# Placing VectorE's sum for the last down product behind the block's last output sum

## The chip, the cores and the metric

The kernel runs on one core of a Trainium2 chip. The metric is the device time of one execution in microseconds (us). One execution was also taken by the hardware profiler; its page and its trace are what this document reads. Engines are named as there: PE is TensorE's matmuls, PEld its weight loads, DVE is VectorE, ACT ScalarE, POOL GpSimd, SP SyncE. L12 is line 12 of the kernel.

## What is computed

Two stages follow each other: a filter in the frequency domain along the sequence of each of 8 batches, and a two-layer network with a hardswish between its layers on every one of the 8 x 3008 = 24064 tokens.

```python
X = np.fft.rfft(x, axis=1)                    # x: (8, 3008, 256)
Y = X * (filt_r + 1j * filt_i)[None]
x = np.fft.irfft(Y, n=3008, axis=1).reshape(24064, 256)
h = x @ w_in                                  # (256, 2048)
g = h * np.clip(h + 3.0, 0.0, 6.0) / 6.0
out = g @ w_out                               # (2048, 256)
```

All data is float32.

## The kernel before, in words

The network runs in 47 blocks of 512 tokens (`NBLK`, k = 0 to 46). A block runs through its 2048 hidden columns in 8 parts (`NP`, p = 0 to 7) of 256. One step of the main loop is one (k, p): it does the up products of (k, p) and the down products of the part before it, (kd, pd). The filter of the next batches is cut into units (`b_unit`, `f_unit`, `y_unit`, `bi3_unit`, `n_unit` and others), and a plan made ahead of the loop sets which unit runs in which step, at one of three places in it, `do(0)`, `do(1)` and `do(2)`. The order of instructions on every engine is the order in which the program issues them; nothing is reordered by a scheduler.

Each 2 x 2 block product is done with seven products in place of eight (in Strassen's manner), so sums are needed in front and behind.

- Up, products by their weights: A11, S1 and A12 (`up_1`), S2 and S4 (`up_2`), S3 (`up_3`), A22 (`up_5`). They accumulate in two PSUM tiles, `al` and `be`. VectorE makes h0 from them in `up_2b` (L790) and the upper half of h1 in `up_3` (L795); ScalarE copies the lower half of h1 (L804) and makes the two relus (L809). A22 writes into `al`, so its weight load waits until h1's addition has read it.
- Hardswish: `hswish(k, p, 0)` and `hswish(k, p, 1)` (L814) write G11 with G3's first content, and G12 with G22. The second is issued in the next step, at the head of `g_sums`.
- VectorE's sums for the down products: `g_sums` makes G1 (L821), then G3 and G2 (L822); `g_last` makes G4 = G12 - G2 (L827). G4 is read by down product 3 alone.
- Down: seven products numbered 1 to 7, each of two matmuls of 128 columns, each of these done as two loads and two matmuls in the trace (L843). In one step they come as 1; 2 and 4; 5 and 6; 7 and 3. They accumulate over the 8 parts of a block in four PSUM banks, `po0` to `po3`: products 1 and 4 in bank 0, 2 and 6 in bank 1, 5 in bank 2, 7 and 3 in bank 3. Products 1, 2, 5 and 7 open their banks in the first part of a block.
- The block's sums: when a block's last part is through, ScalarE and VectorE take the four banks apart into the output tile `o`. `out_1` (ScalarE, L900), `out_2` and `out_3` (VectorE, L909 and L914) run in the step with pd = 7; `out_4` (two VectorE sums, L918 and L919, and a GpSimd sum, L920) and `out_5` (one VectorE sum, L923, that reads the second half of bank 3) run in the step after it, whose pd is 0. `out_5` ends with `store(kd - 1)`, which issues the DMAs of that block's output from SP. There are 45 such steps with kd > 1; they have p = 1.

`g_last` has two places. In a step that is `late(i)` it comes directly behind h1's addition, in others in front of product 1. `late` holds for every step with p = 1 or 2, and for steps behind one with a heavy unit:

```python
        def late(i):
            return i % NP in (1, 2) or any(fn in HEAVY for place in range(3) for fn, a in plan.get((i - 1, place), ()))
```

So in the 45 steps VectorE's order is: hswish 1 of the part before, G1, G3 and G2, the two sums of `out_4`, h0, h1, G4 (`g_last`), `out_5`, hswish 0. TensorE's order is: `up_1`, units of `do(0)`, product 1, `up_2`, products 2 and 4, `up_3`, products 5 and 6, units of `do(1)`, `up_5` (A22), products 7 and 3.

GpSimd makes the seven sums of the next block's inputs in `t_sums` (L760), whenever ScalarE has copied them (`ready`), and the one sum of `out_4`.

The main loop (in the function that the diff touches) and what calls it:

Of the kernel before, what the change touches and what calls it, by code (L numbers as in the profile page):

```python
# [182 lines left out]
def kernel(  # L183
# [582 lines left out]
    def up_1(k, p):  # L766
        t = st["xt", k]
        al = psU.tile([P, 512], FP32, name="al")[:, 0:256]
        be = psU.tile([P, 512], FP32, name="be").rearrange("p (a n) -> p a n", a=2)
        s = hp.tile([P, 2, 256], FP32, name="s")  # L770
        s5 = hp.tile([P, 256], FP32, name="s5")
        product(al, p, A11, t[:, F1, :], start=True)
        product(be[:, 1, :], p, S1, xb(k, 0, 1), start=True)
        product(be[:, 0, :], p, A12, t[:, F4, :])
        nc.scalar.activation(out=s[:, 0, :], in_=al, func=AXT.Copy)  # L775
        nc.scalar.activation(out=s5, in_=be[:, 1, :], func=AXT.Copy)  # L776
        st["up"] = al, be, s, s5
# [10 lines left out]
    def up_2b(k, p):  # L788
        al, be, s, s5 = st["up"]
        nc.vector.tensor_tensor(out=st["h"][0].rearrange("p (a n) -> p a n", a=2), in0=be, in1=s, op=ALU.add)  # L790
# [26 lines left out]
    def g_sums(k, p):  # L817
        hswish(k, p, 1)
        g = st["g", k, p]
        v = nc.vector  # L820
        v.tensor_tensor(out=g[:, G1, :], in0=g[:, G3, :], in1=g[:, G22, :], op=ALU.add)  # L821
        v.tensor_tensor(out=g[:, G3:G2 + 1:2, :], in0=g[:, G3:G1 + 1, :],  # L822
                        in1=g[:, G11:G11 + 1, :].broadcast_to([P, 2, 256]), op=ALU.subtract)

    def g_last(k, p):
        g = st["g", k, p]
        nc.vector.tensor_tensor(out=g[:, G4, :], in0=g[:, G12, :], in1=g[:, G2, :], op=ALU.subtract)  # L827
# [7 lines left out]
    def down(k, p, *prods):  # L835
        g = st["g", k, p]
        if p == 0 and 1 in prods:
            st["po", k] = [psO.tile([P, 2, 2, P], FP32, name="po%d" % i) for i in range(4)]
        for n in prods:
            bank, part = BANK[n]  # L840
            a, w = DOWN[n]
            for u in range(2):
                nc.tensor.matmul(st["po", k][bank][:, part, u, :], g[:, a, ts(u, P)], w_out[p][:, w, :],  # L843
                                 start=(p == 0 and n in OPENS and u == 0), stop=(p == NP - 1 - (k == LAST)),
                                 skip_group_check=True)

    def last_down():
        p, v, add = NP - 1, nc.vector.tensor_tensor, ALU.add
        g, o = st["g", LAST, p], st["o", LAST][0]
        hswish(LAST, p, 1)  # L850
        ps = [psF.tile([P, 512], FP32, name="psf", tag="f") for t in range(2)]
        for i, a in ((0, G11), (1, G12)):
            for t in range(2):
                for u in range(2):
                    nc.tensor.matmul(ps[t][:, ts(u, D)], g[:, a + t, ts(u, P)],
                                     w_out[p][:, 2 * i:2 * i + 2, :].rearrange("p j m -> p (j m)"),
                                     start=i == 0 and u == 0, stop=i == 1, skip_group_check=True)
        out_4(LAST)
        v(out=o_at(LAST, 0, 1), in0=st["po", LAST][3][:, 1, :, :], in1=o_at(LAST, 0, 1), op=add)
        for t, qs in ((0, (nc.sync, nc.gpsimd, nc.scalar)), (1, (nc.sync, nc.scalar))):  # L860
            both = o[:, t, :, :].rearrange("p u d -> p (u d)")
            v(out=both, in0=ps[t], in1=both, op=add)
            store_last(t, qs)
# [6 lines left out]
    def plain_up(p):  # L870
        st["g", 0, p] = gp.tile([P, 7, 256], FP32, name="g")
        st["h"] = [psU.tile([P, 512], FP32, name=n) for n in ("al", "be")]
        for i in range(2):
            for d in range(2):
                nc.tensor.matmul(st["h"][i], w_in[p][:, 2 * d + i, :], xn[:, d, :, 0:PAIRS], start=d == 0, stop=d == 1)  # L875
            relu(i)
            hswish(0, p, i)

    def plain_down(p, tokens=(0, 1)):
        g = st["g", 0, p]  # L880
        if p == 0:
            st["po", 0] = [psO.tile([P, 2, 2, P], FP32, name="po%d" % i) for i in range(2)]
        for t in tokens:
            for u in range(2):
                for i, a in ((0, G11), (1, G12)):
                    nc.tensor.matmul(st["po", 0][t][:, u, :, :].rearrange("p a m -> p (a m)"), g[:, a + t, ts(u, P)],  # L886
                                     w_out[p][:, 2 * i:2 * i + 2, :].rearrange("p j m -> p (j m)"),
                                     start=p == 0 and u == 0 and i == 0, stop=p == NP - 1, skip_group_check=True)
# [14 lines left out]
    def o_at(k, t, d):  # L903
        return st["o", k][0][:, t, :, ts(d, P)]
# [17 lines left out]
    def out_5(k):  # L922
        nc.vector.tensor_tensor(out=o_at(k, 0, 1), in0=st.pop(("po", k))[3][:, 1, :, :], in1=o_at(k, 0, 1), op=ALU.add)  # L923
        store(k)
# [20 lines left out]
    def store(k):  # L945
        o = st["o", k][0]
        nc.sync.dma_start(o_d[ds(k * PAIRS, PAIRS)].rearrange("(u p) d -> p u d", p=P), o[:, 1, :, :])
        for u, p, m, b_, j, a in runs(k):
            for h in range(1 if j else 2):
                nc.sync.dma_start(raw(out, b_ * N + row(j, h, a), [[NC * D, m], [1, D]]), o[p:p + m, h, u, :])  # L950
        for b_, r, j, m, na in BACK.get(k, ()):
            to, half = out.offset + (b_ * N + N - j) * D, D // 2
            a0, a1 = ([[D, m], [-NC * D, na], [1, D]], [[NA * D, m], [D, na], [1, D]]) if m > 1 else (
                [[half, 2], [-NC * D, na], [1, half]], [[half, 2], [D, na], [1, half]])
            nc.sync.dma_start(bass.AP(tensor=out.tensor, offset=to, ap=a0),
                              bass.AP(tensor=o_d.tensor, offset=o_d.offset + r * D, ap=a1))
# [21 lines left out]
    with tc.manual_schedule():  # L978
# [207 lines left out]
        def late(i):  # L1186
            return i % NP in (1, 2) or any(fn in HEAVY for place in range(3) for fn, a in plan.get((i - 1, place), ()))

        items = [(k, p) for k in range(NBLK) for p in range(NP)]
        for i in range(len(items) + 1):  # L1190
            up = i < len(items)
            k, p = items[min(i, len(items) - 1)]
            dn = i > 0
            kd, pd = items[i - 1]
            def do(place):
                for fn, a in plan.get((i, place), ()):
                    fn(*a)

            if k == 0:
                plain_up(p)  # L1200
                do(0)
                if dn:
                    plain_down(pd)
                do(1)
                do(2)
                continue
            if not up:
                last_down()
                break
            up_1(k, p)  # L1210
            ends = k == LAST and p == NP - 1
            do(0)
            last_plain = dn and kd == 0
            dn = dn and kd > 0
            if dn:
                g_sums(kd, pd)
                if not late(i):
                    g_last(kd, pd)
                down(kd, pd, 1)
            if up:  # L1220
                up_2(k, p)
            if dn and pd == 0 and kd > 1:
                out_4(kd - 1)
            if up:
                up_2b(k, p)
            if dn:
                down(kd, pd, 2, 4)
                if pd == NP - 1:
                    out_1(kd)
            if up:  # L1230
                up_3(k, p)
                if dn and late(i):
                    g_last(kd, pd)
            if dn:
                down(kd, pd, 5, 6)
            if up:
                up_4(k, p)
            if ends:
                out_1(k)
            if last_plain:  # L1240
                plain_down(pd, (0,))
            if dn and pd == 0 and kd > 1:
                out_5(kd - 1)
            if up:
                hswish(k, p, 0)
                do(1)
            if up:
                up_5(k, p)
            bi3_copies()
            if last_plain:  # L1250
                plain_down(pd, (1,))
                plain_out()
            if dn:
                if pd == NP - 1 or ends:
                    out_2(kd)
                down(kd, pd, 7, 3)
                if pd == NP - 1 or ends:
                    out_3(kd)
            do(2)
# [30 lines left out]
```

## Time and profile before

| what | value |
|---|---|
| median of 3 runs | 2656.8 us (2656.7 to 2656.96) |
| the profiled execution's own time | 2656.55 us |
| its span in the profile | 2654.7 us |
| mean granted TensorE clock | 0.999 |
| DVE L827 (`g_last`), 367 times | 414 / 415 / 943 ns (least, median, most) |
| DVE L923 (`out_5`), 45 times | 411 / 419 / 424 ns |
| DVE L795 (h1), 368 times | 425 ns mean |
| POOL L760, sums of `xn` / of `xt` | 757 / 932 ns mean |

The page gives busy times and shares of the span by engine, the chain of work that ended last, and groups of instructions by line with their mean length and the idle time ahead of them. Two more views are used. The waits list who waited for whom, in total, how often, and the longest. The timeline lists instructions in order of time: start from the span's beginning, length, engine, line, operation, output and inputs, how many instructions are merged in the row, and in brackets the idle time in front of it with what ended it. Lengths of neighbours can overlap by some hundredths of a microsecond, since an engine starts an instruction while the one before is finishing. The ends of matmuls are modelled, so TensorE's pace is better read from the starts of its weight loads.

### The profile page before, as it was taken

To read this page: it belongs to the slowest core of one execution; us is meant where nothing else is said; L and a number is where in the kernel's file an instruction comes from. 1 tells how busy PE (TensorE), PEld (TensorE's weight loads), DVE (VectorE), ACT (ScalarE), POOL (GpSimd) and SP (SyncE) were. 2 spreads that over 40 slices of the span, in tenths; PEclk is the share of its full clock that TensorE was granted. 3 is DMA by queue.
4 is the path that set the end of the run, shared out by engine and by line. 5 is a ranking of instruction groups with operands and counts; after the bars stand their busy time and mean duration, and the time that the engine had idled before them with its cause. 6 is when DMAs were issued, how large, how long until landed. Compare 5 with 4: busy or idle time off the path is not lost.

```text
span 2654.7 us, 54856 instructions
## 1 busy us (share of the span) xinstructions
PE 2638.6 (99%) x21872; PEld 2334.1 (88%) x21872; DVE 2038.2 (77%) x3602; ACT 1298.6 (49%) x2682; POOL 484.3 (18%) x707
## 2 busy tenths in 40 slices
PE   8999999999999999999999999999999999999999
PEld 6688888889889898898988988889888888999998
DVE  7878767887678876788767887688877878766666
ACT  4554454444544444444444544545445444454554
POOL 2242021120211102121021210211112120111110
PEclk9999999999999999999999999999999999999999
DMA  9732234112241133411333112331223321110000
GB/s 248 219 92 71 72 84 115 52 32 82 79 116 52 32 85 81 111 52 36 80 88 104 52 37 80 89 103 52 56 61 88 103 56 48 48 43 22 19 20 25
DMA packets 130646, 198.29 MB, mean 75 GB/s; under 512 B 21538, under 2 KB 97408, under 8 KB 130198
## 3 DMA queue, kind: packets, MB, share of 16 engines
q1 hardware_dynamic: 115165, 150.12, 20.7%
q0 software_dynamic: 14656, 44.16, 6.0%
q8 instruction: 173, 2.83, 0.5%
q14 instruction: 83, 0.68, 0.1%
q10 hardware_dynamic: 569, 0.50, 0.1%
HBM read 122.43 MB, written 83.98 MB: 78 GB/s over the span
## 4 chain that ended last, share of the span: by engine, by line
PE 97%; DVE 2%; DMA 1%; issue 0%; ACT 0%; SPq 0%; POOL 0%; POOLq 0%; DVEq 0%
PE po L843 43%; PE al L764 24%; PE be L764 18%; PE psn L704 2%; PE psf L539 1%; PE psf L480 1%; PE po L886 1%; PE be L599 1%; PE psf L599 1%; PE be L480 1%; PE psf L583 0%; DMA w_all<-in_x_dram 0%; PE al L875 0%; PE be L875 0%; DVE g L814 0%; PE po L548 0%
## 5 line engine op out<-in xcount | busy, mean ns | idle before, releaser
L843 PEld LDWEIGHTS po<-w_all,g 128*128 128x128 f32 x10276 | 1366.4, 191 | 121.1 <-issue 20.3
L843 PE MATMUL po<-w_all,g 128*128 128x128 f32 x10276 | 1396.7, 276 | 1.2 <-DVE g L814 0.6
L809 ACT ACTIVATE r<-h,half_c 128x512 f32<-128x512 f32 x736 | 531.0, 721 | 334.1 <-DVE h L790 322.0
L764 PE MATMUL al<-xt,w_all 128*128 128x256 f32 x2208 | 659.7, 381 | 0.1
L814 DVE SCALAR_TENSOR_TENSOR g<-r,h 128x512 f32<-128x512 f32 x736 | 530.1, 720 | 159.8 <-ACT r L809 144.7
L764 PE MATMUL be<-xt,w_all 128*128 128x256 f32 x1472 | 437.8, 379 | 0.0
L790 DVE TENSOR_TENSOR h<-be,s 128x512 f32<-128x512 f32 x368 | 253.8, 690 | 157.3 <-PE be L764 148.6
L764 PEld LDWEIGHTS al<-xt,w_all 128*128 128x128 f32 x2208 | 335.5, 192 | 1.0 <-issue 0.5
L764 PEld LDWEIGHTS be<-xt,w_all 128*128 128x128 f32 x1472 | 279.8, 190 | 37.8
L760 POOL TENSOR_TENSOR xt<-xn 128x256 f32<-128x256 f32 x184 | 135.9, 757 | 876.7 <-ACT xn L686 842.6
L804 ACT ACTIVATE h<-al 128x256 f32<-128x256 f32 x368 | 141.0, 383 | 299.8 <-PE al L764 299.8
L795 DVE TENSOR_TENSOR h<-al,s 128x256 f32<-128x256 f32 x368 | 156.3, 425 | 157.4 <-PE al L764 154.1
L822 DVE TENSOR_TENSOR g<-g 128x512 f32<-128x512 f32 x367 | 261.3, 712 | 12.6
L785 ACT ACTIVATE s<-al 128x256 f32<-128x256 f32 x368 | 141.1, 383 | 211.9 <-PE al L764 210.4
L764 PE MATMUL al<-xn,w_all 128*128 128x256 f32 x736 | 226.1, 389 | 0.0
L776 ACT ACTIVATE s<-be 128x256 f32<-128x256 f32 x368 | 141.1, 383 | 172.2 <-PE be L764 172.2
L764 PE MATMUL be<-xn,w_all 128*128 128x256 f32 x736 | 218.9, 379 | 0.0
L821 DVE TENSOR_TENSOR g<-g 128x256 f32<-128x256 f32 x367 | 167.5, 456 | 12.6
L775 ACT ACTIVATE s<-al 128x256 f32<-128x256 f32 x368 | 140.8, 383 | 71.7 <-PE al L764 71.7
L764 PEld LDWEIGHTS be<-xn,w_all 128*128 128x128 f32 x736 | 139.9, 190 | 18.9
L827 DVE TENSOR_TENSOR g<-g 128x256 f32<-128x256 f32 x367 | 154.6, 421 | 2.5
L920 POOL TENSOR_TENSOR o<-p,o 128x256 f32<-128x256 f32 x46 | 36.8, 799 | 602.8 <-DVE o L918 557.4
(171 smaller groups left out, 1933.5 us busy)
## 6 DMA issues: line engine op xcount, KB each, us to landing
t<-g_tmp SPq DMA_DIRECT2D x184, 120.0 KB
t<-z_tmp SPq DMA_DIRECT2D x42, 512.0 KB
g_tmp<-t POOLq DMA_DIRECT2D x72, 256.0 KB, 5.5
z_tmp<-t POOLq DMA_DIRECT2D x120, 144.0 KB, 3.4
o_tmp<-o SPq DMA_DIRECT2D x46, 256.0 KB
xs<-in_x_dram SPq DMA_DIRECT2D x60, 192.0 KB
ft<-in_filt_r_dram SPq DMA_DIRECT2D x168, 64.0 KB
ft<-in_filt_i_dram SPq DMA_DIRECT2D x168, 64.0 KB
```

What stands on the lines that cost most here:

```text
L764: nc.tensor.matmul(ps, w_in[p][:, w, :], x, start=start, stop=stop, skip_group_check=True)
L776: nc.scalar.activation(out=s5, in_=be[:, 1, :], func=AXT.Copy)
L785: nc.scalar.activation(out=s[:, 1, :], in_=al, func=AXT.Copy)
L790: nc.vector.tensor_tensor(out=st["h"][0].rearrange("p (a n) -> p a n", a=2), in0=be, in1=s, op=ALU.add)
L795: nc.vector.tensor_tensor(out=st["h"][1][:, 256:512], in0=al, in1=s5, op=ALU.add)
L804: nc.scalar.activation(out=st["h"][1][:, 0:256], in_=al, func=AXT.Copy)
L809: nc.scalar.activation(out=r, in_=st["h"][i], func=AXT.Relu, bias=half_c, scale=1.0 / 6.0)
L814: nc.vector.scalar_tensor_tensor(out=st["g", k, p][:, o:o + 2, :].rearrange("p a n -> p (a n)"), in0=st["r", i], scalar=1.0, in1=st["h"][i ...
L821: v.tensor_tensor(out=g[:, G1, :], in0=g[:, G3, :], in1=g[:, G22, :], op=ALU.add)
L822: v.tensor_tensor(out=g[:, G3:G2 + 1:2, :], in0=g[:, G3:G1 + 1, :], in1=g[:, G11:G11 + 1, :].broadcast_to([P, 2, 256]), op=ALU.subtract)
L827: nc.vector.tensor_tensor(out=g[:, G4, :], in0=g[:, G12, :], in1=g[:, G2, :], op=ALU.subtract)
L843: nc.tensor.matmul(st["po", k][bank][:, part, u, :], g[:, a, ts(u, P)], w_out[p][:, w, :], start=(p == 0 and n in OPENS and u == 0), stop= ...
```

## The change

In the 45 steps that have `out_5` in them, `g_last` is issued behind `out_5` (and behind the store that `out_5` ends with) in place of directly behind h1's addition. Every other step keeps its order. On VectorE the order h1, G4, `out_5`, hswish 0 becomes h1, `out_5`, G4, hswish 0. No instruction is added or left out.

```diff
@@ -1229,7 +1229,7 @@
                     out_1(kd)
             if up:
                 up_3(k, p)
-                if dn and late(i):
+                if dn and late(i) and not (pd == 0 and kd > 1):
                     g_last(kd, pd)
             if dn:
                 down(kd, pd, 5, 6)
@@ -1241,6 +1241,7 @@
                 plain_down(pd, (0,))
             if dn and pd == 0 and kd > 1:
                 out_5(kd - 1)
+                g_last(kd, pd)
             if up:
                 hswish(k, p, 0)
                 do(1)
```

## Prediction

> **What bounds the kernel now.** First the page: busy shares, then the chain that ended last.
>
> ```profile
> PE 2638.6 (99%) x21872; PEld 2334.1 (88%) x21872; DVE 2038.2 (77%) x3602; ACT 1298.6 (49%) x2682; POOL 484.3 (18%) x707
> PE 97%; DVE 2%; DMA 1%; issue 0%; ACT 0%; SPq 0%; POOL 0%; POOLq 0%; DVEq 0%
> ```
>
> TensorE is the bound, so only its waits matter. Busy time hides short ones; the waits of the weight loads (PEld) show them:
>
> ```profile
> PEld po L843 <- PE po L843: 10.3, 32, 0.3
> ```
>
> 32 times a load of a down product stood 0.32 us. The timeline of the weight loads in block 9 (start, length, engine, line) says where:
>
> ```profile
> 593.98 0.30 PEld L764 LDWEIGHTS al<-xn,w_all 128*128 128x128 f32 x2
> 594.60 0.97 PEld L843 LDWEIGHTS po<-w_all,g 128*128 128x128 f32 x8 [0.32 <-PE po L843]
> 595.49 0.30 PEld L764 LDWEIGHTS al<-xt,w_all 128*128 128x128 f32 x2
> ...
> 600.32 0.30 PEld L764 LDWEIGHTS al<-xn,w_all 128*128 128x128 f32 x2
> 600.64 1.08 PEld L843 LDWEIGHTS po<-w_all,g 128*128 128x128 f32 x8
> 601.64 0.30 PEld L764 LDWEIGHTS al<-xt,w_all 128*128 128x128 f32 x2
> ```
>
> al<-xn is product A22 (up_5), the eight loads are down products 7 and 3, the next al<-xt opens the next step. In the step after (p=2) it goes 600.32, 600.64, 601.64: 1.32 us. In step p=1, where the change is, it goes 593.98, 594.60, 595.49: 1.51 us. Product 7's load comes 0.30 late, and 0.19 of it stays, since a load otherwise starts 0.11 before its matmul can. VectorE at that place:
>
> ```profile
> 593.40 0.42 DVE L795 TENSOR_TENSOR h<-al,s 128x256 f32<-128x256 f32 x1 [0.56 <-PE al L764]
> 593.74 0.41 DVE L827 TENSOR_TENSOR g<-g 128x256 f32<-128x256 f32 x1
> 594.07 0.42 DVE L923 TENSOR_TENSOR o<-po,o 128x256 f32<-128x256 f32 x1
> 594.40 0.88 DVE L814 SCALAR_TENSOR_TENSOR g<-r,h 128x512 f32<-128x512 f32 x1
> 595.89 1.22 DVE L814 SCALAR_TENSOR_TENSOR g<-r,h 128x512 f32<-128x512 f32 x1 [0.61 <-ACT r L809]
> ...
> 599.04 0.68 DVE L790 TENSOR_TENSOR h<-be,s 128x512 f32<-128x512 f32 x1
> 599.73 0.42 DVE L795 TENSOR_TENSOR h<-al,s 128x256 f32<-128x256 f32 x1
> ```
>
> L923 (out_5) ends at 594.49; product 7, which reopens the PSUM bank that out_5 reads, loads at 594.60. Going through all 45 places, 33 loads stand 0.115 us behind out_5's end. The releaser in brackets, an older matmul, is a misreading: in block 7 out_5 ends 0.53 us later than usual (485.40) and the load stands at 485.52. In the other 12 blocks a bi3_unit lies ahead of A22, out_5 is over 1.6 us early, and the sequence takes 1.32 us.
>
> **What the Trainium skill says.** "SBUF — State Buffer", section "Who interferes with whom": a VectorE instruction with two SBUF inputs and a GpSimd instruction that reads SBUF exclude each other for a whole instruction; one with at most one SBUF input is free. The trace agrees: L923 and L795 take 0.42 whether GpSimd runs or not, while L814 takes 0.68 alone and 0.88 or 1.22 beside it, and L827 0.41 or 0.94. "TensorE: Matmul & The Clock Gate", "Step-by-step: what each phase is for": loads of weights are pulled ahead of running matmuls. Here by 0.11 us, so a late load costs less than its lateness. "Perfetto Trace Analysis", "Identifying Dependency Chains": an instruction that waits for several engines can have an event-semaphore instruction put before it. That fits product 7, which waits on two counters: 0.115 us from out_5's end, against 0.05 where a load waits on VectorE alone (block 3, A22: 266.34 to 266.39). No page's price is used below.
>
> **The change, part by part.** It swaps two VectorE instructions, g_last (L827, writes G4, needed by product 3) and out_5 (L923), in 45 steps. Nothing is added: VectorE's sum of both stays, as they run head to tail.
>
> (a) out_5 takes g_last's slot: start to start 0.33 earlier. Product 7's load may then go at 594.60 - 0.33 = 594.27; TensorE's own pace puts it at 593.98 + 0.33 = 594.31, and up to 0.11 later would still cost nothing. The stall goes: 0.188 us each (1.513 - 1.325), in 32 steps, and 2.040 - 1.325 = 0.715 in block 7. Ceiling: 32 x 0.188 + 0.715 = 6.7 us.
>
> (b) g_last ends 0.33 later, where out_5 ended: 594.49, ready at 594.54. Product 3's first load is due 0.55 after product 7's, at 594.86. What hides it is product 7's four matmuls: 0.32 of room. Without them it would cost what it is late, as the loads of one product after another run at the matmuls' own pace of 0.11.
>
> (c) What is moved past: ScalarE's relu(0), whose input is ready anyway; the allocation of the next g; and the DMAs of store(kd-1), which SP issues once out_5 has ended. They start 0.33 earlier; no engine waits for them. Nothing of GpSimd's queue is crossed. hswish(k,p,0) stays third.
>
> (d) GpSimd. Its row in block 9:
>
> ```profile
> 593.85 2.02 POOL L760 TENSOR_TENSOR xt<-xt 128x256 f32<-128x256 f32 x2
> 595.84 0.72 POOL L760 TENSOR_TENSOR xt<-xn 128x256 f32<-128x256 f32 x1
> ```
>
> In 17 of the 33 blocks (2, 3, 6, 7, 9, 12, 13, 15, 18, 19, 21, 24, 25, 27, 30, 31, 36) t_sums runs here. Now g_last gets the port first, and GpSimd's sum is stretched by 0.15 (0.88 for 0.73). After the change out_5 needs no port, GpSimd takes it, and ends at 593.85 + 0.73 = 594.58; g_last gets it then and ends 0.28 later, 594.86 (block 7 shows this today: L827 ends 0.28 behind GpSimd's end). Ready at 594.92: product 3 is 0.06 late, and TensorE gains 0.13.
>
> From there the two take turns, 0.59 per GpSimd sum and 0.55 per L814, as between 595.87 and 599.11 today: GpSimd to 595.45, hswish 0 to 596.00 (now 595.28; product 1 loads it at 596.68), GpSimd to 596.59, hswish 1 to 597.14 (now 597.11; product 2 loads it at 597.99). VectorE is then 0.03 to 0.04 behind today while TensorE is 0.13 ahead.
>
> Does the next step bear that? In 7 of the 17 (2, 6, 12, 18, 24, 30, 36) other matmuls lie there and h1's addition has 0.56 us idle before it: it does. In 8 (9, 13, 15, 19, 21, 25, 27, 31) it has 0.016 (L795 at 599.73 shows none), and A22's load follows it by 0.16 where 0.05 is the least: 0.12 of room, less 0.04. Such a block keeps about 0.08; worked out one by one with the start of GpSimd's sum in each, they keep 0.05 to 0.19, together 0.8.
>
> In block 3, y_unit's two long sums follow: with one more turn ahead of them hswish 1 ends at 264.55 for 263.81, product 2 (due 263.97) loads at 264.60, 0.11 of that is caught up, and another 0.11 is room that A22's own wait there leaves today: -0.4. In block 7 nothing of VectorE moves after out_5 and g_last, and product 2 then waits for hswish 1 (487.33, load 487.39 for 487.60): it keeps 0.21 + 0.11 = 0.3.
>
> **Sum.** 16 quiet blocks 16 x 0.188 = 3.0; 7 x 0.125 = 0.9; 8 blocks 0.8; block 3 -0.4; block 7 0.3: 4.6 us. The profiled execution took 2656.55 (span 2654.7, 1.9 outside it): 2652.0. The median is 0.25 above it, so 2652.2, 0.17% less. About 0.2% (5.3 us) is what a measurement of this kernel can tell from no change.
>
> **Bounds.** The unknown is the turn-taking, which no row shows for this order. Best end: it costs nothing, -6.7. Worst on this side: it eats all of the gain in the 17 blocks and block 3 its 0.4, -2.6. I take the turns as today's rows show them.
>
> **Rivals.**
> 1. The port costs nothing: GpSimd's sum, now earlier, leaves g_last in time, and the next step has room. For: 0.06 is little. Against: L827 at 0.94 in block 7, and 8 blocks with 0.016 idle. 6.7 us: 2650.1. Chance 0.20.
> 2. The gain in contended blocks is given back in the next step by VectorE (late hswish 1, late h1): 3.0 - 0.4 = 2.6 us: 2654.2. For: block 9's unbroken row of VectorE. Against: only 8 blocks have it. Chance 0.15.
> 3. Product 7 waits for TensorE's own counter, as the bracket says, and nothing moves: 2656.8. Against: block 7 and the 12 free blocks. Chance 0.04.
> 4. Slower: g_last loses two turns in a row to GpSimd in 16 contended blocks. It then ends 0.59 later, product 3 waits 0.65, a step loses 0.65 - 0.19 = 0.46: 16 x 0.46 = 7.4 against 3.0 + 0.3 gained, 4.1 slower: 2660.9. It decides from a wait of 0.40, that is a g_last of over 1.1 us; the longest of 367 is 0.94, after one turn. Chance 0.04.
>
> **How the numbers follow.** The forecast has 0.57, its own range 2651.3 to 2652.9; about an eighth of it lies below 2651.5. Faster by over 0.2%: 0.20 + 0.07 = 0.27. Slower: 0.04. Within: 0.69. A range of 2649.9 to 2654.0 holds the forecast, rival 1 and the nearer part of rival 2, and leaves out under 0.2.
>
> **What would show it.** L923 right behind L795, L827 behind it; the 32 waits of 0.32 gone; A22 to the next A11 at 1.32 in quiet blocks (5, 11, 41 to 46) and about 1.39 in block 9; L827 at about 0.8 to 0.9 in contended blocks, with a wait of product 3 on it; A22 waiting for h1 in p=2 of the 8 blocks; block 3 longer. Wrong if product 7 still stands behind out_5, if contended blocks also show 1.32 and no wait for h1 (rival 1), or if L827 goes over 1.1 us (rival 4).

## The result, and the profile after

The changed kernel takes 2651.79 us (median of 15 runs, 2650.05 to 2652.93) against 2657.08 us before (15 runs, 2655.45 to 2658.80). The ratio is 0.998 with a 95% interval of 0.9972 to 0.9987: faster by 0.13 to 0.28%. The forecast was 2652.2. The profiled execution took 2651.27 us where the one before took 2656.55; its span went from 2654.7 to 2649.5.

The page first: busy shares, and the chain that ended last, by engine.

```profile
PE 2634.2 (99%) x21872; PEld 2338.2 (88%) x21872; DVE 2045.6 (77%) x3602; ACT 1299.8 (49%) x2682; POOL 484.2 (18%) x707
PE 96%; DMA 2%; DVE 2%; issue 0%; SPq 0%; ACT 0%; POOL 0%; POOLq 0%; DVEq 0%
```

The same number of instructions, TensorE as full as before. VectorE is busy 7.4 us longer (2045.6 for 2038.2). This isn't work: the time is added in `g_last` (L827, busy 160.1 for 154.6) and in hswish (L814, 534.1 for 530.1), in the 17 blocks where GpSimd's sums run beside them. There they stand at the port that VectorE shares with GpSimd; no other VectorE line changes by more than 0.5. The row of 32 waits of 0.32 us in front of a down product is not in the waits of the weight loads any more. Block 9, the timeline of the weight loads (start, length, engine, line, instruction):

```profile
593.39 0.30 PEld L764 LDWEIGHTS al<-xn,w_all 128*128 128x128 f32 x2
593.72 1.12 PEld L843 LDWEIGHTS po<-w_all,g 128*128 128x128 f32 x8
594.76 0.30 PEld L764 LDWEIGHTS al<-xt,w_all 128*128 128x128 f32 x2
```

A22 at 593.39, product 7 at 593.72: the stall is gone. But the next step's A11 comes at 594.76, 1.37 behind A22 where 1.32 is the pace, and the eight loads take 1.12 in place of 1.08: product 3 waited a little. VectorE and GpSimd at that place:

```profile
592.81 0.42 DVE L795 TENSOR_TENSOR h<-al,s 128x256 f32<-128x256 f32 x1 [0.56 <-PE al L764]
593.15 0.41 DVE L923 TENSOR_TENSOR o<-po,o 128x256 f32<-128x256 f32 x1
593.48 0.78 DVE L827 TENSOR_TENSOR g<-g 128x256 f32<-128x256 f32 x1
594.18 2.34 DVE L814 SCALAR_TENSOR_TENSOR g<-r,h 128x512 f32<-128x512 f32 x2
...
598.45 0.68 DVE L790 TENSOR_TENSOR h<-be,s 128x512 f32<-128x512 f32 x1
599.05 0.41 DVE L795 TENSOR_TENSOR h<-al,s 128x256 f32<-128x256 f32 x1
```

```profile
593.25 0.73 POOL L760 TENSOR_TENSOR xt<-xt 128x256 f32<-128x256 f32 x1
...
594.81 1.17 POOL L760 TENSOR_TENSOR xt<-xn 128x256 f32<-128x256 f32 x1
```

L923 stands in front of L827 now. The first of GpSimd's sums starts at 593.25 and is no longer stretched: it takes 0.73, to 593.98. `g_last` takes 0.78 where it took 0.41, and ends at 594.26, 0.28 behind that sum.

Where the 5.2 us of span went can be read without the runs' spread. The distances from one A22 weight load to the next are nearly the same in two traces of one kernel (the changed one and its repetition r4: all but nine of 367 to 5 ns, the worst to 17), so they give the gain step by step.

| steps (us; negative is faster) | forecast | changed kernel |
|---|---|---|
| 16 blocks without GpSimd's sums there | -3.0 | -3.03 |
| 7 blocks with them and other matmuls in the next step | -0.9 | -0.94 |
| 8 blocks with them and a bare next step | -0.8 | -1.18 |
| block 3 | +0.4 | +0.43 |
| block 7 | -0.3 | -0.72 |
| the other 13 blocks | 0 | -0.08 |
| sum | -4.6 | -5.50 |

The head of the kernel, up to block 1, took 0.34 us longer in this execution; -5.50 and 0.34 are the 5.2 of the span. Between the ten profiled executions of this study the head differs by up to 1.9 us, and no edit touches it. The runs of one kernel spread by 3 us; the head is the only part in which two traces of one kernel (the changed one and r4) differ by more than 0.1 us.

### The profile page after: what moved, and what is told of

Its sections match the earlier page's. It is cut to its first block, busy times and chain, and to the rows that moved or that the text cites. A ratio compares the mean times of both kernels' runs of the same rounds, so it can differ in the third digit from the quotient of the medians.

```text
span 2649.5 us, 54856 instructions
## 1 busy us (share of the span) xinstructions
PE 2634.2 (99%) x21872; PEld 2338.2 (88%) x21872; DVE 2045.6 (77%) x3602; ACT 1299.8 (49%) x2682; POOL 484.2 (18%) x707
## 4 chain that ended last, share of the span: by engine, by line
PE 96%; DMA 2%; DVE 2%; issue 0%; SPq 0%; ACT 0%; POOL 0%; POOLq 0%; DVEq 0%
PE po L843 43%; PE al L764 24%; PE be L764 18%; PE psn L704 2%; PE psf L539 1%; PE psf L480 1%; PE po L886 1%; PE be L599 1%; PE psf L599 1%; PE psf L583 1%; PE be L480 1%; DVE g L814 0%; PE al L875 0%; PE be L875 0%; DMA ft<-in_filt_i_dram 0%; PE po L548 0%
## 5 line engine op out<-in xcount | busy, mean ns | idle before, releaser
L814 DVE SCALAR_TENSOR_TENSOR g<-r,h 128x512 f32<-128x512 f32 x736 | 534.1, 727 | 151.9 <-ACT r L809 135.8
L790 DVE TENSOR_TENSOR h<-be,s 128x512 f32<-128x512 f32 x368 | 253.6, 689 | 153.0 <-PE be L764 144.5
L760 POOL TENSOR_TENSOR xt<-xn 128x256 f32<-128x256 f32 x184 | 142.7, 795 | 874.1 <-ACT xn L686 840.3
L795 DVE TENSOR_TENSOR h<-al,s 128x256 f32<-128x256 f32 x368 | 156.0, 424 | 156.7 <-PE al L764 156.1
L827 DVE TENSOR_TENSOR g<-g 128x256 f32<-128x256 f32 x367 | 160.1, 436 | 2.5
L920 POOL TENSOR_TENSOR o<-p,o 128x256 f32<-128x256 f32 x46 | 36.7, 799 | 602.4 <-DVE o L918 557.1
```

The source lines that it names most:

```text
L760: nc.gpsimd.tensor_tensor(out=o, in0=x0, in1=x1, op=op_)
L795: nc.vector.tensor_tensor(out=st["h"][1][:, 256:512], in0=al, in1=s5, op=ALU.add)
L814: nc.vector.scalar_tensor_tensor(out=st["g", k, p][:, o:o + 2, :].rearrange("p a n -> p (a n)"), in0=st["r", i], scalar=1.0, in1=st["h"][i ...
```

## The experiments

What a step gained or lost is taken from the traces as in the table. The diffs of r1, r2, r7 and r8 are against the changed kernel, that of r5 is against r2's; r3 and r6 make the same edits as r2 and r5, to the kernel before. Lines left out are marked with `...`.

**r1, out_5 between h0's and h1's addition.** `g_last` goes back to its old place; `out_5` is moved ahead instead.

```diff
             if up:
                 up_2b(k, p)
+            if dn and pd == 0 and kd > 1:
+                out_5(kd - 1)
...
-                if dn and late(i) and not (pd == 0 and kd > 1):
+                if dn and late(i):
                     g_last(kd, pd)
...
-            if dn and pd == 0 and kd > 1:
-                out_5(kd - 1)
-                g_last(kd, pd)
```

> out_5 is issued between h0's and h1's addition, where VectorE idles 0.56 us for TensorE (0.30 in block 3), and g_last keeps its old place directly behind h1. Theory (product 7 stands behind out_5; what the change lost, it lost because g_last came later and met GpSimd's sum): all 33 steps with a stall go to 1.32 us from A22 to the next step, in blocks with t_sums running too, L827 is as long as in the kernel before (0.41, 0.94 in block 7), block 3's product 2 doesn't wait; block 3 gains nothing. 31 x 0.188 + 0.715 = 6.5 us under the kernel before, about 1 us under the changed kernel. Rival (what counts is the distance from h1's addition, so that out_5 in front of it delays h1, A22 and the lower half of h1): A22 comes 0.1 to 0.3 later in each of the 45 steps, and 4 to 13 us of the gain are lost.

Measured: 2649.53 us against 2657.32, ratio 0.9972 (0.9961 to 0.9983): faster than the kernel before. The changed kernel, measured again on the same chip (r4), took 2651.59. That difference, 2.1 us, has no interval on record; 1.8 of it is in the steps of the two traces (r1 and r4).

> The changed kernel once more, on the same chip as the others, to compare them with: 5.2 us under the kernel before, the same lengths of its steps to a few ns, and differences of up to about 1.5 us between runs that come from the head of the kernel, not from its steps.

r4's ratio was 0.9979 (0.997 to 0.9987), its step sums within 0.1 us of the first trace's, and its head 0.67 us shorter than that one's. r1's VectorE and weight loads in block 9:

```profile
590.66 0.69 DVE L790 TENSOR_TENSOR h<-be,s 128x512 f32<-128x512 f32 x1 [1.26 <-PE be L764]
591.27 0.41 DVE L923 TENSOR_TENSOR o<-po,o 128x256 f32<-128x256 f32 x1
591.92 0.42 DVE L795 TENSOR_TENSOR h<-al,s 128x256 f32<-128x256 f32 x1 [0.23 <-PE al L764]
592.26 0.41 DVE L827 TENSOR_TENSOR g<-g 128x256 f32<-128x256 f32 x1
```

```profile
592.50 0.30 PEld L764 LDWEIGHTS al<-xn,w_all 128*128 128x128 f32 x2
592.83 1.08 PEld L843 LDWEIGHTS po<-w_all,g 128*128 128x128 f32 x8
593.82 0.30 PEld L764 LDWEIGHTS al<-xt,w_all 128*128 128x128 f32 x2
```

h1 still had 0.23 idle behind `out_5`, so it came no later, `g_last` met GpSimd exactly as before the change, and A22 to A11 is 1.32. The 31 ordinary steps gained 0.188 each, block 7 0.716, block 3 nothing, as expected: 6.6 us. Unexpected: 0.8 us more came from the other blocks, 0.10 in each of seven. There hswish 0 now comes 0.33 earlier on VectorE, and so no longer holds up the two-column copy behind it (L601, of the `bi3_unit` in that step). In block 10 the copy comes 0.11 earlier in its step, and the weight load that follows it stands 0.05 behind its end in both traces.

**r2 and r3, t_sums issued later.** The 17 blocks' `t_sums` moves from step p=1 to p=3 or 5, on top of the changed kernel (r2) and of the kernel before (r3).

```diff
-            t_sums(t // PAIRS)
+            (st["due"].append if "due" in st else t_sums)(t // PAIRS)
...
+            if k in (2, 3, 6, 7, 9, 12, 13, 15, 18, 19, 21, 24, 25, 27, 30, 31, 36):
+                if p == 0:
+                    st["due"] = []
+                if p == (5 if k in (2, 3, 6, 12, 18, 24, 30, 36) else 3):
+                    for q in st.pop("due"):
+                        t_sums(q)
             up_1(k, p)
```

> The changed kernel, with GpSimd's seven sums for the next block (t_sums) issued in step p=3 or 5 in place of p=1 in the 17 blocks where they ran beside out_5 and g_last. Theory (port turns of GpSimd and VectorE make g_last late there, and hswish 1 in block 3): L827 takes 0.41 in all 45 steps, all take 1.32 us from A22 to the next step, block 3 no longer waits 0.77 for product 2: 17 steps x 0.05 to 0.09 and 0.4 to 0.6 for block 3, 1.3 to 1.7 us under the changed kernel, less what the sums cost where they now run. Rival (the rest of the stall is not GpSimd's): steps stay at 1.37 to 1.42 in these blocks, and the time doesn't move.

> The kernel before, with t_sums issued in step p=3 or 5 in the same 17 blocks: the suspected contention alone is taken away, the order is the old one. Theory: the stall in front of product 7 stays at 0.188 in all 33 steps, since out_5 still comes behind g_last; only block 7, where GpSimd stretched g_last by 0.53, falls from 0.715 to 0.188: 0.5 us faster, no more. Rival (GpSimd's sums make the stall): several us faster.

Measured: r2 2651.46 us (ratio 0.998, 0.9971 to 0.9988), r3 2658.09 (1.0003, 0.9995 to 1.0012). Neither tested what it was to test: the edit moved the sums in the program and not in time. GpSimd in block 9 of r2:

```profile
589.70 0.73 POOL L920 TENSOR_TENSOR o<-p,o 128x256 f32<-128x256 f32 x1 [44.85 <-DVE o L918]
590.70 2.10 POOL L760 TENSOR_TENSOR xt<-xn 128x256 f32<-128x256 f32 x3 [0.27 <-ACT xn L686]
592.88 1.58 POOL L760 TENSOR_TENSOR xt<-xt 128x256 f32<-128x256 f32 x2
```

The sums still begin in step p=1, as soon as their input is copied; only L920 has passed them. GpSimd's queue runs as far ahead as its waits let it. Where that swap moved GpSimd's phase, the steps moved too: in r3 `g_last` took 0.90 and 0.95 in blocks 2 and 3, and these two cost 0.48 and 0.52 us more.

**r5 and r6, t_sums held.** As r2 and r3, and GpSimd now first does an added subtraction of two columns, which reads the G11 of the step before, so that the sums behind it can't start earlier.

```diff
-                        t_sums(q)
+                        t_sums(q, st["g", k, p - 1][:, G11, 0:2])
...
-    def t_sums(k):
+    def t_sums(k, hold=None):
         t = xtp.tile([P, 5, PAIRS], FP32, name="xt")
+        if hold is not None:
+            nc.gpsimd.tensor_tensor(out=t[:, F1, 0:2], in0=hold, in1=hold, op=ALU.subtract)
```

> The changed kernel, with t_sums in the 17 blocks issued in step p=3 or 5 and held there: GpSimd first does a subtraction of two columns of the G11 that VectorE writes in the step before, so it can't run ahead. Theory (port turns of GpSimd and VectorE make g_last late): L827 takes 0.41 in all 45 steps, all 33 take 1.32 us from A22 to the next step, block 3's product 2 doesn't wait. The 17 blocks gain 3.5 us in place of 2.4: about 1.1 us under the changed kernel, less what the sums cost in the steps to which they go (0 to 1). Rival (the rest of the stall has another cause): the steps stay at 1.37 to 1.42 there.

> The kernel before, with t_sums held in the same way: the contention alone is taken away. Theory: the stall ahead of product 7 stays at 0.188 in every one of the 33 steps, since out_5 still comes behind g_last; only block 7 falls from 0.715 to 0.188, and block 3 may gain 0.1: 0.5 to 0.7 us faster in the loop, within what a measurement can tell. Rival (GpSimd's sums make the stall): the 17 steps fall to 1.32, about 3.5 us faster.

Measured: r5 2660.82 us against 2656.81 (ratio 1.0015, 1.0009 to 1.0022), r6 2666.89 (1.0038, 1.0026 to 1.0051). Block 9 of r5 (line numbers are higher by two), with the changed order, and of r6, with the old one:

```profile
592.55 0.30 PEld L766 LDWEIGHTS al<-xn,w_all 128*128 128x128 f32 x2
592.88 1.08 PEld L845 LDWEIGHTS po<-w_all,g 128*128 128x128 f32 x8
593.88 0.30 PEld L766 LDWEIGHTS al<-xt,w_all 128*128 128x128 f32 x2
...
607.00 0.13 PEld L599 LDWEIGHTS be<-y,wi 64*64 64x64 f32 x1 [0.90 <-DVE t L601]
```

```profile
594.31 0.30 PEld L766 LDWEIGHTS al<-xn,w_all 128*128 128x128 f32 x2
594.93 0.97 PEld L845 LDWEIGHTS po<-w_all,g 128*128 128x128 f32 x8 [0.32 <-PE po L845]
595.82 0.30 PEld L766 LDWEIGHTS al<-xt,w_all 128*128 128x128 f32 x2
```

In r5 all 45 steps take 1.32 from A22 to A11, block 3's product 2 waits for nothing and that block turns from +0.43 into -0.28. In r6 the wait of 0.32 is still there in all 33 steps; only block 7 falls, by 0.53, and block 3 by 0.11. So GpSimd's sums make neither the stall nor its end; they make what is lost of the gain. With the sums out of the way, the change by itself is worth 6.1 us (2660.82 for 2666.89), and 33 x 0.188 is 6.2.

The total of r5 was expected 1 us under the changed kernel and is 9 us over it: the expectation's "0 to 1" for the sums' new place was far too low. Nine blocks lose 1.0 us each in p=3 and six lose 0.2 in p=5. In the six, the turns at the port make h1's addition late, and A22 waits for it (block 6: the addition ends at 455.28, the load stands at 455.33). For the nine, the row at 607.00 says where: a `bi3_unit`'s matmuls wait for its two-column copy L601, and on VectorE that copy stands behind a hswish 0 of 1.21:

```profile
605.66 1.21 DVE L816 SCALAR_TENSOR_TENSOR g<-r,h 128x512 f32<-128x512 f32 x1
606.80 0.15 DVE L601 COPY t<-be 128x2 f32<-128x2 f32 x1
```

**r7, g_last one place further, behind hswish 0.**

```diff
             if dn and pd == 0 and kd > 1:
                 out_5(kd - 1)
-                g_last(kd, pd)
             if up:
                 hswish(k, p, 0)
+                if dn and pd == 0 and kd > 1:
+                    g_last(kd, pd)
                 do(1)
```

> One place further: h1, out_5, hswish 0, g_last. Theory (product 3 has 0.32 us of room behind product 7, and g_last takes a turn for each sum it lets ahead): in quiet blocks G4 is ready 0.60 later, 0.28 past the room, so a step loses 0.28 of the 0.19 it had gained; in contended ones g_last comes after another turn of GpSimd and product 3 waits about 1.2. 16 x 0.09 + 16 x 1.0 = 17 us slower than the kernel before, about 2674. Rival (product 3's place leaves enough room, or its loads don't hold up what follows): like the changed kernel, 2652.

Measured: 2675.20 us against 2656.81 (ratio 1.007, 1.0056 to 1.0083). The weight loads in a quiet block, 5:

```profile
375.77 0.30 PEld L764 LDWEIGHTS al<-xn,w_all 128*128 128x128 f32 x2
376.10 0.63 PEld L843 LDWEIGHTS po<-w_all,g 128*128 128x128 f32 x4
376.93 0.52 PEld L843 LDWEIGHTS po<-w_all,g 128*128 128x128 f32 x4 [0.20 <-DVE g L827]
```

Product 7 goes at once, product 3 (the second four loads) waits for L827. Quiet steps are 0.09 longer than before the change, contended ones 0.87 to 1.03 (block 7 only 0.30): 0.09 and 1.0 had been worked out. Not worked out was what five of the 12 other blocks lose (8, 14, 20, 26, 38), 0.22 each, 1.1 us together. There the copy L601 stands behind `g_last` now, and the matmuls of the `bi3_unit` wait for it: in block 8 it comes 0.23 later in its step, and the load 0.05 behind it.

**r8, the opposite of the change: h1, g_last, hswish 0, out_5.**

```diff
-                if dn and late(i) and not (pd == 0 and kd > 1):
+                if dn and late(i):
                     g_last(kd, pd)
...
+            if up:
+                hswish(k, p, 0)
             if dn and pd == 0 and kd > 1:
                 out_5(kd - 1)
-                g_last(kd, pd)
             if up:
-                hswish(k, p, 0)
                 do(1)
```

> The opposite of the change: h1, g_last, hswish 0, out_5. Theory (product 7 stands 0.115 us behind out_5's end): in quiet blocks its load comes 0.60 later than before, 0.79 of stall per step in place of 0.19; in contended ones, where hswish 0 takes a turn, about 1.15 later; the 12 blocks with a bi3_unit stay as they are. 16 x 0.60 + 16 x 1.15 + about 0.8 = 29 us slower than before, 2686. Rival (product 7 waits for TensorE's own counter): no change, 2657.

Measured: 2686.85 us against 2656.81 (ratio 1.0114, 1.0098 to 1.0129). VectorE and the weight loads in block 5:

```profile
374.68 0.68 DVE L814 SCALAR_TENSOR_TENSOR g<-r,h 128x512 f32<-128x512 f32 x1
375.28 0.42 DVE L923 TENSOR_TENSOR o<-po,o 128x256 f32<-128x256 f32 x1
```

```profile
374.59 0.30 PEld L764 LDWEIGHTS al<-xn,w_all 128*128 128x128 f32 x2
375.81 0.30 PEld L843 LDWEIGHTS po<-w_all,g 128*128 128x128 f32 x2 [0.92 <-PE al L764]
```

`out_5` ends at 375.70 and the load goes at 375.81, again 0.11 behind it. Quiet steps are 0.60 longer than before, contended ones 1.13 (block 3 1.02). The bracket, here as in the kernel before, names an older matmul. The trace of before has the reason: right ahead of the load an event-semaphore instruction (594.53 in block 9), which the timeline leaves out, waits for VectorE's counter, and the load itself waits for TensorE's alone. The 12 blocks with a `bi3_unit` did not all stay as they were: the same five as in r7 lose 0.21 each, as L601 now stands behind `out_5`.

## Why the prediction held, point by point

**The total.** 4.6 us less was forecast; the loop gained 5.5, and the medians are 5.3 apart. That 2652.2 lies only 0.4 from 2651.79 is in part luck: it was reckoned from 2656.8 for the kernel before, which came to 2657.08 in the larger set of runs.

**(a) The stall.** Right, in mechanism and size. All 33 loads of product 7 that stood behind `out_5` stand no more, and the quiet blocks gained 0.188 each. Rival 3 (TensorE's own counter) is out: r8 moves the load with `out_5` alone.

**(b) The room of product 3.** Right: 0.32 in quiet blocks. r7 oversteps it by what was worked out, 0.28, and pays that.

**(c) What was moved past** cost nothing that shows: the quiet steps gain the full 0.188.

**(d) GpSimd's turns.** Right, and shown by r5 against the changed kernel: without the sums there, no step pays. The seven blocks gained 0.127 to 0.141 (0.125 forecast), `g_last` took 0.78 in block 9 (0.79 was implied: 594.07 to 594.86 on the old time scale), block 3 lost 0.43 (0.4 forecast), with product 2 waiting for hswish 1:

```profile
263.63 0.41 PEld L764 LDWEIGHTS be<-xt,w_all 128*128 128x128 f32 x2
264.80 0.97 PEld L843 LDWEIGHTS po<-w_all,g 128*128 128x128 f32 x8 [0.77 <-DVE g L814]
```

Two terms of the sum were too small a gain, and together they are 0.8 of the 0.9 us by which the forecast fell short in the loop.

**Block 7: 0.72 for 0.3.** The forecast took the loads at 487.60 for product 2. They are product 1. The trace of before:

```profile
487.60 0.63 PEld L843 LDWEIGHTS po<-w_all,g 128*128 128x128 f32 x4
488.15 0.30 PEld L764 LDWEIGHTS al<-xt,w_all 128*128 128x128 f32 x2
488.48 0.41 PEld L764 LDWEIGHTS be<-xt,w_all 128*128 128x128 f32 x2
488.91 1.08 PEld L843 LDWEIGHTS po<-w_all,g 128*128 128x128 f32 x8
```

Four loads are one product; the eight at 488.91, behind S2 and S4, are products 2 and 4. hswish 1 was over at 487.33, 1.6 us ahead of them, so nothing was there to take the gain.

**The eight bare blocks: 1.18 for 0.8.** The forecast gave h1's addition 0.016 us of room, the idle time in front of L795. The real room was larger: idle time is counted from the end of the record in front, and L795 can start before L790's record ends. In block 9 before, L795 started 0.695 behind L790's start with 0.016 idle; held by nothing but VectorE, it starts 0.600 behind, as in block 9 after (598.45 to 599.05). So 0.095 could be given up, not 0.016. With the 0.10 in front of A22 (0.12 in the forecast) that is 0.2, no less than the 0.10 to 0.19 by which TensorE was ahead, and A22 waited in none of the eight. The evidence was in the trace of before: in block 3 L790 and L795 stood at 265.32 and 265.93. And in block 9 it was TensorE that set L795's time: 599.73 is 0.74 behind the first load of S3, and so is every L795 of before that has idle time in front of it:

```profile
598.99 0.30 PEld L764 LDWEIGHTS al<-xt,w_all 128*128 128x128 f32 x2
```

Idle time can miss such a wait altogether. In block 7 after, L795 again stands 0.74 behind S3's load and 0.67 behind L790, which is 0.07 more than VectorE needs, and no idle time is shown:

```profile
489.31 0.30 PEld L764 LDWEIGHTS al<-xt,w_all 128*128 128x128 f32 x2
```

```profile
489.39 0.68 DVE L790 TENSOR_TENSOR h<-be,s 128x512 f32<-128x512 f32 x1
490.06 0.42 DVE L795 TENSOR_TENSOR h<-al,s 128x256 f32<-128x256 f32 x1
```

**The rivals.** Of the rivals, rival 1 (no cost of the port) came nearest in the total, 1.7 us below what was measured, and is wrong in its reason: 14 of the contended steps are longer than 1.32, and r1, which takes that cost away, gains another 1.1 us in these 17 blocks. Rival 2 (given back in the next step) held in block 3 alone. Rival 4's price is real, since r7 puts `g_last` behind two more turns, hswish 0's and another of GpSimd's, and loses 1.0 a step; but `g_last` directly behind `out_5` waited for one sum of GpSimd's alone.

## What to carry to other kernels

When an instruction of a side engine holds up the bound engine, look for the idle time ahead of it on the side engine first: moving `out_5` into a gap of 0.56 us, where VectorE waited anyway (r1), cost no step anything, while swapping it with its neighbour cost that neighbour a turn at GpSimd's port in 17 blocks. An instruction that needs no port, put in front of one that does, gives the other engine time to take the port first: behind `out_5`, `g_last` went from 0.41 to 0.78 us in block 9. And moving an instruction in the program moved it in time only where something in its own queue held it (r5 and r6, not r2 and r3).

## What had not been expected of the hardware

- The idle time in front of a VectorE instruction understates how far it could be moved up, by 0.08 us here: L790's record is 0.68 long, and L795 can start 0.600 behind its start. So L795 had 0.016 of idle time and 0.095 of room.
- The turns at the port, which the forecast had taken from a few rows, were strict wherever both engines had work queued: 0.58 to 0.60 for a GpSimd sum of 128x256, 0.55 for a VectorE product of 128x512, 0.28 for a sum of 128x256, one after the other. In the 17 contended blocks of the changed kernel that is 153 turns, with no engine going twice in a row.
- A two-column copy of 0.15 us (L601) held TensorE's loads for 0.9 us where it stood behind a stretched instruction (r5).
